# A linear-attention and max-out network kernel: the bonus of the third chunk by corner products, twelve more products of zeros at the start, and a new table of due times

## The chip, the cores and the metric

One NeuronCore of a Trainium2 chip runs the whole program. The metric is device time in microseconds; three runs of the kernel before are known, and one more execution was profiled. TensorE (PE) multiplies, VectorE (DVE), ScalarE (ACT) and GpSimd (POOL) do element work, and SyncE (SP) issues nearly all transfers.

## The reference, cut to what matters

```python
for t in range(S):                         # S = 768, B = 4, H = 8, D = 48
    cur = einsum('bhd,bhe->bhde', u[None] * k[t], v[t])          # the bonus of the own token
    y[t] = einsum('bhd,bhde->bhe', r[t], state + cur)
    state = w[None, :, :, None] * state + einsum('bhd,bhe->bhde', k[t], v[t])
x = y as (3072, 384)
h = maximum(maximum(x @ w1, x @ w2), x @ w3)                     # 384 -> 768
out = h @ w_out                                                  # 768 -> 384
```

## The kernel before, in words

The 768 tokens are cut into 12 chunks of 64. For each chunk the attention forms scores (keys against receptances, 64x64 for each of 32 pairs of batch and head), masks them to the earlier tokens, and multiplies them with the values (`va` in the plan) and the receptances with the running state; `ke` is the product that renews the state. Each chunk is done in two halves, q = 0 and 1. Behind the attention of a chunk comes its network: for six slices f of the hidden layer three products `up` of nine matmuls (128x256, float16), the maximum of the three on ACT and DVE, and then the products `dn`. The float64 weights come as halves (`word`), are turned into float16 high and low parts by DVE and ACT (lines 319 to 330), and an `up` needs the parts of its slice.

Chunks 0 to 3 (`WHOLE`) take the attention in float32 with 64x64 corners of TensorE (`corner`, line 563); from chunk 4 on it is float16 high and low parts (line 476), spread over block-diagonal tiles by transfers.

The score of a token with itself needs the bonus u, and there are two ways to it. In chunks 0 and 1 (`EARLY`) ACT multiplies the keys by u (`rated`, line 485), TensorE forms a second set of corners `bo`, and `mask_bonus` (line 490) copies its diagonal into the tile `amz`, which is zeroed once and used by all early chunks; `mask` (line 502) then copies the scores of earlier tokens into it. In the other chunks the diagonal is made from the token-major tensors: `product` (lines 457 and 458: r times u, times k), `total` (line 462: a sum over 48), and `diagonal` (line 466: spread on the eye), on DVE or POOL, and `mask` goes on top.

Nothing is ordered by the code's own sequence. Every step is given to `Plan.do` with a due time, an engine, a cost, what it reads and writes, and the pools from which it takes buffers. `Plan.order` then fills the engines greedily by these costs, and the steps are recorded in that order, so each engine runs its own list in order. `SHIFT` moves the due times of each kind of step in five stages of the program. A product of zeros (`stir`, line 626) runs on TensorE in four places: once before any data is there, and three times between the first products.

Loads of chunks 0 to 3 go into tiles that later hold spread operands (`blocks[...]room`, named by `FEATS` and `TOKS`) or, where `TOKS` has None, into the pool `tok` of three buffers: halves 2/0, 2/1 and 3/0 fill it in the kernel before.

Of the kernel before, what the change touches and what calls it, by code (L numbers as in the profile page):

```python
# [29 lines left out]
EARLY = (0, 1)  # L30
FEATS, TOKS = ("kd", "kb", "ktd", "ktb"), ("sd", "vb", None, None)
# [15 lines left out]
class Plan:  # L47
# [11 lines left out]
        "act tkl": (0, -13.11, 0, 0, 0), "act tkt": (0, 50.28, 0, 0, 0), "act vdh": (0, 0, 0, -105.14, -53.73), "act wsq": (0, 0, 0, 0, 5.11),
        "act x": (-47.33, 85.49, 26.22, -20.76, -8.91), "act xh": (-44.75, 0, -100.57, -28.3, -1.81), "act xsq": (0, 15.62, 0, -43.66, -14.22),  # L60
        "act ztop": (0, 54.65, 0, 0, 0), "dve a": (0, 0, -5.17, 101.87, 25.76), "dve al": (0, 0, 0, 60.55, 12.26, 0, 0, 0, -22.37, 7.04),
        "dve am": (0, 0, 10.09, -12.88, 8.82, 0, 0, -0.23, -2.17, -8.37), "dve amz": (-64.19, -80.08, -13.83, -77.16, 0),
        "dve ends": (0, 0, 0, 149.19, 0), "dve flag": (0, 0, 0, 0, 113.54), "dve good": (0, 0, 0, 0, 32.48),
        "dve hl": (0, -19.31, 58.16, -54.83, -18.79, 0, 1.9, 5.29, -9.39, 0.06),
        "dve kT": (-10.41, -22.95, 4.53, -23.13, -0.12, -5.93, 16.46, -7.26, 21.08, 0.27),
        "dve kdec": (0, 10.74, 3.61, -55.17, -3.05, 0, 2.89, -4.71, 5.85, 6.5), "dve kdl": (0, 0, 0, 28.7, 76.75, 0, 0, 0, 12.53, -8.95),
        "dve ktdl": (0, 0, 0, -75.87, 22.48, 0, 0, 0, -22.66, 3.88), "dve lo": (0, -60.79, 0, 0, 0), "dve m": (0, -79.26, -57.34, -93.14, 22.59),
        "dve rT": (0.88, -19.98, -13.12, 14.62, -30.28, 11.81, 1.66, -8.46, -9.57, 8.77), "dve rl": (0, 0, 0, -95.56, 15.83, 0, 0, 0, -27.84, 18.29),
        "dve sdl": (0, 0, 0, -36.04, -22.46), "dve state": (0, 14.9, -58.41, 7.59, 26.82), "dve vdl": (0, 0, 0, 26.05, 13.41),
# [148 lines left out]
def kernel(ctx, tc, feat, tok, wu, ut, ws, wo, cst, vz, out):  # L218
# [615 lines left out]
    def weight(n, h, due):  # L834
# [350 lines left out]
```

## Time and profile before

| what | us |
|---|---|
| three runs | 400.0, 399.22, 397.24 |
| median | 399.22 |
| the profiled execution | 398.11 |
| its span, first to last instruction | 395.7 |
| TensorE busy | 375.1 |
| VectorE busy | 256.2 |
| ScalarE busy | 211.2 |
| GpSimd busy | 157.3 |

A busy time is a mean over stages with different limits: TensorE is busy for 95% of the span, but some of that is zeros and some of it ran at half the clock. The rows below show stretches of time, and the granted clock (1.00 is 2.4 GHz, 0.50 is 1.2 GHz) stands in its own column.

### The profile page before, as it was taken

The numbers are of one execution on the slowest core, as the hardware profiler recorded it, in microseconds if no ns is written. First come the engines' busy times: TensorE is split into PE (matmuls) and PEld (weight loads), VectorE is DVE, ScalarE is ACT, GpSimd is POOL, SyncE is SP. The second block draws the span as 40 slices with busy tenths as digits, with TensorE's granted clock in tenths as the row PEclk, the third lists the DMA queues.
The fourth block names the chain that finished last, engine by engine and source line by source line (L and its number), as shares of the span: only waits on it lengthen the run. The fifth ranks groups of instructions, "written<-read, shape, count | busy, mean of one in ns | idle before, by whom it ended". The sixth has DMA issues, their size and how long they took to land.

```text
span 395.7 us, 12676 instructions
## 1 busy us (share of the span) xinstructions
PE 375.1 (95%) x5256; PEld 337.2 (85%) x5256; DVE 256.2 (65%) x495; ACT 211.2 (53%) x532; POOL 157.3 (40%) x154
## 2 busy tenths in 40 slices
PE   6979499899999999999999999899999999999996
PEld 5868398688889998899998899799899999988885
DVE  5629989997646766934377449789467668243441
ACT  4335174676457676544444448457349738922421
POOL 7366764313365839730465116156019104000000
PEclk9999889999999999999999999999999999999999
DMA  7996329964639797876516892994995894420101
GB/s 267 411 407 209 130 67 315 258 221 118 174 92 274 200 244 193 244 198 181 162 59 165 206 288 72 257 277 117 240 314 140 196 250 107 120 65 7 41 3 45
DMA packets 28271, 72.55 MB, mean 183 GB/s; under 512 B 4849, under 2 KB 12081, under 8 KB 28209
## 3 DMA queue, kind: packets, MB, share of 16 engines
q1 hardware_dynamic: 28064, 71.59, 63.5%
q8 instruction: 43, 0.70, 0.8%
q14 instruction: 20, 0.16, 0.2%
q10 hardware_dynamic: 144, 0.10, 0.1%
HBM read 35.97 MB, written 4.72 MB: 103 GB/s over the span
## 4 chain that ended last, share of the span: by engine, by line
PE 72%; DMA 10%; DVE 5%; issue 4%; ACT 3%; SPq 3%; POOL 1%; DVEq 0%; POOLq 0%
PE psm L630 55%; PE psa L563 9%; PE psa L476 8%; DMA ktb<-ktd 4%; DMA sb<-sd 3%; SPq L559 2%; DVE m L649 1%; PE psm L626 1%; DMA feat<-in_feat_dram 1%; DMA kd<-in_feat_dram 1%; DVE raw L323 1%; ACT junk L426 1%; DVE tok L472 1%; DVE hl L655 1%; DMA x<-x 1%
## 5 line engine op out<-in xcount | busy, mean ns | idle before, releaser
L630 PEld LDWEIGHTS <-w 128*128 128x128 f16 x2592 | 250.1, 98 | 33.5 <-issue 2.4
L630 PE MATMUL psm<-x,w 128*128 128x256 f16 x1944 | 220.8, 273 | 3.5 <-DVE m L649 2.5
L649 DVE SCALAR_TENSOR_TENSOR m<-psm,m 128x256 f32<-128x256 f32 x144 | 60.0, 419 | 48.8 <-PE psm L630 46.3
L652 ACT CAST hh<-m 128x256 f16<-128x256 f32 x72 | 28.7, 400 | 54.6 <-DVE m L649 53.9
L630 PE MATMUL psm<-hh,w 128*128 128x256 f16 x432 | 55.8, 273 | 0.0
L655 POOL TENSOR_TENSOR hl<-m,hh 128x256 f16<-128x256 f32 x25 | 17.9, 718 | 85.4 <-ACT hh L652 81.7
L457 POOL TENSOR_TENSOR am<-tok,u_sb 128x384 f32<-128x384 f32 x19 | 22.5, 1185 | 45.8 <-DVE al L512 45.8
L645 ACT ACTIVATE m<-psm 128x256 f32<-128x256 f32 x72 | 27.0, 377 | 24.1 <-PE psm L630 22.8
L630 PE MATMUL psm<-hl,w 128*128 128x256 f16 x216 | 33.4, 273 | 0.0
L554 DVE SCALAR_TENSOR_TENSOR x<-psa,x 128x512 f16<-128x512 f32 (+1 forms) x24 | 16.2, 677 | 26.4 <-ACT x L548 26.2
L655 DVE TENSOR_TENSOR hl<-m,hh 128x256 f16<-128x256 f32 x47 | 24.0, 514 | 8.7 <-ACT hh L652 8.7
L426 ACT ACTIVATE junk<-tok 128x384 bf16<-128x384 f32 x48 | 24.9, 519 | 5.2 <-DMA tok<-in_tok_dram 4.4
L466 POOL TENSOR_TENSOR am<-cs,a 128x512 f32<-128x512 f32 x19 | 21.7, 1140 | 14.9 <-DVE a L462 8.7
L675 ACT ACTIVATE io<-psm 128x256 f32<-128x256 f32 x36 | 12.9, 382 | 26.4 <-PE psm L630 26.4
L438 POOL TENSOR_TENSOR feat<-feat,wrt 128x512 f32<-128x512 f32 x12 | 17.1, 1423 | 21.4 <-DMA feat<-in_feat_dram 21.4
L476 PE MATMUL psa<-rh,sb 128*128 128x64 f16 x256 | 23.6, 193 | 2.0 <-DMA sb<-sd 2.0
L502 DVE COPY_PREDICATED am<-cs,psa 128x512 f32<-128x512 int32 x20 | 14.5, 731 | 16.4 <-PE psa L476 15.5
L548 ACT ACTIVATE x<-psa 128x512 f16<-128x512 f32 (+1 forms) x24 | 14.1, 585 | 20.1 <-PE psa L476 16.4
L476 PE MATMUL psa<-ah,vb 128*128 128x64 f16 x256 | 23.9, 193 | 0.1
L476 PE MATMUL psa<-al,vb 128*128 128x64 f16 x128 | 22.8, 193 | 0.0
L476 PE MATMUL psa<-rl,sb 128*128 128x64 f16 x128 | 22.7, 193 | 0.0
L476 PEld LDWEIGHTS <-sb 128*128 128x128 f16 x384 | 20.0, 98 | 2.2 <-DMA sb<-sd 1.5
(138 smaller groups left out, 572.9 us busy)
## 6 DMA issues: line engine op xcount, KB each, us to landing
tok<-in_tok_dram SPq DMA_DIRECT2D x20, 576.0 KB, 7.5
feat<-in_feat_dram SPq DMA_DIRECT2D x16, 512.0 KB, 6.6
raw<-in_ws_dram SPq DMA_DIRECT2D x12, 576.0 KB, 6.5
out_dram<-io SPq DMA_DIRECT2D x36, 128.0 KB, 3.4
kb<-kd SPq DMA_DIRECT2D x16, 256.0 KB, 4.4
kb<-kd SPq DMA_DIRECT2D x16, 248.0 KB, 4.5
vb<-vd SPq DMA_DIRECT2D x16, 224.0 KB, 5.2
sb<-sd SPq DMA_DIRECT2D x16, 224.0 KB, 5.7
```

Source lines behind the costliest of these rows:

```text
L426: nc.scalar.activation(out=junk[:, 0:U * D].rearrange("p (u d) -> p u d", u=U), in_=src, func=AF.Square, scale=scale, accum_out=stat[:, ki ...
L438: eng.tensor_tensor(out=t[n], in0=t[n], in1=tb, op=ALU.mult)
L457: eng.tensor_tensor(out=w.rearrange("p (g b) d -> p g b d", g=2), in0=t["r"], in1=by_token(u_sb, q), op=ALU.mult)
L466: eng.tensor_tensor(out=t["a"], in0=eye.unsqueeze(1).broadcast_to([P, U, C]), in1=t.pop("sum").unsqueeze(2).broadcast_to([P, U, C]), op=AL ...
L476: nc.tensor.matmul(out=ps, lhsT=l[i], rhs=rr[j], start=first and n == 0, stop=last and n == 2)
L554: nc.vector.scalar_tensor_tensor(out=lo, in0=src, scalar=x_scale(c), in1=hi, op0=ALU.mult, op1=ALU.subtract)
L563: nc.tensor.matmul(out=ps[hh * C + at:hh * C + at + n, i, :], lhsT=lhs[HS[hh]], rhs=rhs[HS[hh]], start=first, stop=last)
L630: nc.tensor.matmul(out=ps, lhsT=a, rhs=b, start=first and n == 0, stop=last and n == len(prods) - 1)
L645: nc.scalar.mul(out=m, in_=ps, mul=by)
L649: nc.vector.scalar_tensor_tensor(out=m, in0=ps, scalar=by, in1=m, op0=ALU.mult, op1=ALU.max)
L652: nc.scalar.copy(out=h[0][:, f, :], in_=m)
L655: eng.tensor_tensor(out=h[1][:, f, :], in0=m, in1=h[0][:, f, :], op=ALU.subtract)
```

## The change

Chunk 2 is added to `EARLY`, so that its bonus comes by corner products, and its tokens are loaded without r, into the room of the tiles `sb` and not into the pool `tok`. The first run of zeros has 32 products in place of 20. The planner's costs of transfers and of GpSimd change, which changes no instruction but the order of all of them, and every entry of `SHIFT` is new.

```diff
-EARLY = (0, 1)
-FEATS, TOKS = ("kd", "kb", "ktd", "ktb"), ("sd", "vb", None, None)
+EARLY = (0, 1, 2)
+FEATS, TOKS = ("kd", "kb", "ktd", "ktb"), ("sd", "vb", "sb", None)
...
-        "act ah": (0, 0, 0, -114.33, 80.6), "act hh": (0, 36.88, -27.4, -16.07, -13), "act his": (0, -118.51, 0, 0, 0),
+        "act ah": (0, 0, 0, -121.52, 105.27), "act hh": (0, 43, 2.68, -4.11, -0.5), "act his": (0, -53.13, 0, 0, 0),
...
-        do(due, eng, n * Plan.ISSUE[eng] + 0.35 * (n == 2), fn, reads, writes, takes, size + n * 3e4, lanes=n)
+        do(due, eng, n * Plan.ISSUE[eng] + 0.35 * (n == 2), fn, reads, writes, takes, size + n * 4.5e4, lanes=n)
...
-        return ("pool", 0.05 + 2.4e-3 * columns)
+        return ("pool", 0.1 + 2.5e-3 * columns)
...
-        dma(due, fetch, 8 * P * HN, takes=[("raw64", w)])
+        dma(due, fetch, 530842, takes=[("raw64", w)])
...
-            dma(due, lambda: load_feat(c, q), 524288, writes=[f])
+            dma(due, lambda: load_feat(c, q), 356516, writes=[f])
...
-        dma(due, lambda: load_tok(c, q), 589824, takes=[("tok", t)])
+        dma(due, lambda: load_tok(c, q), 513147, takes=[("tok", t)])
...
-        dma(due - 0.22, lambda: spread(nc.sync, kb[q], kd[q], C), 681574, reads=[("kdh", q), ("kdl", q)], writes=[("kb", q)], n=2)
+        dma(due - 0.22, lambda: spread(nc.sync, kb[q], kd[q], C), 558891, reads=[("kdh", q), ("kdl", q)], writes=[("kb", q)], n=2)
...
-        do(due, "pe", 1.0 + 1.0 * q, lambda: values_apart(q), reads=[masked(c, q), ("padded", q), *[("va", c, 0)] * q], writes=[("did", 0, q)] + [("xq", 0)] * q, takes=[("psa", ("va", c, q))])
+        do(due, "pe", 1.0 + 1.55 * q, lambda: values_apart(q), reads=[masked(c, q), ("padded", q), *[("va", c, 0)] * q], writes=[("did", 0, q)] + [("xq", 0)] * q, takes=[("psa", ("va", c, q))])
...
-    do(-9, "pe", 4.3, lambda: stir(20), writes=["warm"], takes=[("psm", "warm")])
+    do(-9, "pe", 5.6, lambda: stir(32), writes=["warm"], takes=[("psm", "warm")])
...
-            for name, tenant, at in (("sd", 0, -0.7), ("kd", 0, -0.4), ("kb", 1, -0.39), ("vd", 0, -0.31), ("vb", 1, -0.3), ("sb", 0, -0.29), ("ktd", 2, -0.2), ("ktb", 3, -0.19)):
+            for name, tenant, at in (("sd", 0, -0.7), ("kd", 0, -0.4), ("kb", 1, -0.39), ("vd", 0, -0.31), ("vb", 1, -0.3), ("sb", 2, -0.29), ("ktd", 2, -0.2), ("ktb", 3, -0.19)):
```

The table of due times decides the order, so its rows are shown as the engines' lists. On VectorE, the stretch before the masks of chunk 2 in the kernel before (`amz` belongs to chunk 1, `am` to chunk 2, `raw` and `w` are weights, `ktb` and `feat` the keys of chunks 3 and 4):

```order
L490 COPY_PREDICATED amz_161<-cs,psa 128x512
L323 SCALAR_TENSOR_TENSOR raw_267<-raw_267,ztop_109 128x576
L502 COPY_PREDICATED amz_161<-cs,psa 128x512
L323 SCALAR_TENSOR_TENSOR raw_270<-raw_270,ztop_110 128x576
L330 SCALAR_TENSOR_TENSOR w_98<-raw_267,w_98 128x576
...
L457 TENSOR_TENSOR am<-tok,u_sb 128x384
L458 TENSOR_TENSOR am<-am,tok 128x384
...
L438 TENSOR_TENSOR ktb_150<-ktb_150,wrt 128x512
L466 TENSOR_TENSOR am<-cs,a 128x512
L438 TENSOR_TENSOR feat<-feat,wrt 128x512
L502 COPY_PREDICATED am<-cs,psa 128x512 x2
```

The same stretch of VectorE in the changed kernel (here `am` and `tok` are chunk 3's, and `amz` serves chunk 1 in rows ahead of `w_98` and chunk 2 behind it):

```order
L323 SCALAR_TENSOR_TENSOR raw_265<-raw_265,ztop_109 128x576
L323 SCALAR_TENSOR_TENSOR raw_301<-raw_301,ztop_110 128x576
L490 COPY_PREDICATED amz_160<-cs,psa 128x512
L490 COPY_PREDICATED amz_161<-cs,psa 128x512
L502 COPY_PREDICATED amz_160<-cs,psa 128x512
L502 COPY_PREDICATED amz_161<-cs,psa 128x512
L330 SCALAR_TENSOR_TENSOR w_98<-raw_265,w_98 128x576
...
L472 TENSOR_TENSOR tok<-tok,tkl 128x384 x2
L490 COPY_PREDICATED amz_160<-cs,psa 128x512
L462 TENSOR_REDUCE a<-am 128x8
L502 COPY_PREDICATED amz_160<-cs,psa 128x512
L554 SCALAR_TENSOR_TENSOR x<-psa,x 128x512
```

The first two conversions of weights stand ahead of chunk 1's masks now, both bonus masks stand ahead of the first score mask, and the mask of chunk 2's first half no longer has a scaling of `ktb`, a `diagonal` and a scaling of `feat` right in front of it.

On SyncE, the loads in the middle of the first stage in the kernel before (`tok` are halves 2/0, 2/1 and 3/0, then 3/1 and 4/0 behind the six small transfers of x; `raw` are weight halves):

```order
L300 DMA raw_348<-in_ws_dram 128x2304
L253 DMA vb_152<-in_tok_dram 128x784
L253 DMA tok<-in_tok_dram 128x1152 x3
L244 DMA ktb_150<-in_feat_dram 128x1024
L244 DMA feat<-in_feat_dram 128x1024
...
L559 DMA x<-x 16x2x256 x6
L253 DMA tok<-in_tok_dram 128x1152 x2
L398 DMA kb_147<-kd_139 64x2048
L399 DMA kb_147<-kd_139 64x1984
L300 DMA raw_1005<-in_ws_dram 128x2304
```

And in the changed kernel (`sb` are halves 2/0 and 2/1, the three of `tok` are 3/0, 3/1 and 4/0):

```order
L300 DMA raw_326<-in_ws_dram 128x2304
L253 DMA vb_152<-in_tok_dram 128x784
L253 DMA sb_153<-in_tok_dram 128x784
L253 DMA sb_154<-in_tok_dram 128x784
L253 DMA tok<-in_tok_dram 128x1152 x3
L244 DMA ktb_150<-in_feat_dram 128x1024
L244 DMA feat<-in_feat_dram 128x1024 x2
...
L559 DMA x<-x 16x2x256 x6
L300 DMA raw_1002<-in_ws_dram 128x2304
L300 DMA raw_1036<-in_ws_dram 128x2304
```

No load of tokens stands behind the transfers of x any more, and the next weight halves follow them directly.

On TensorE the first `up` (`w_98` is the weight tile of slice 0) moves ahead of the scores of chunk 2 and the state product of chunk 1, which stood in front of it before; of the difference, the place behind the values of chunk 1's first half:

```order
 L563 MATMUL psa<-amz_160,vb_151 64x64 x2
 L563 MATMUL psa<-kb_147,state 48x64 x2
+L630 LDWEIGHTS w_98
+L630 MATMUL psm<-x,w_98 128x256
...
 L563 MATMUL psa<-ktd_141 64x64 x16
+L630 LDWEIGHTS w_99
```

Three `up` of slice 0 stand there now ahead of the scores of chunk 2 (`ktd_141`), and three of slice 1 (`w_99`) behind them. The bonus products of chunk 2 follow later, one of them behind the values of chunk 1's second half, since both use the same tile `amz`.

## Rows read from the trace of the kernel before

**Rows 1.** Busy time of each engine by stretch, with granted clock, DMA share, GB/s
```profile
33.81:43.97 10.16, 10.14 (x185) 8.95 (x182) 10.06 (x18) 3.07 (x7) 7.42 (x8) 1.00 0.85 283
43.97:49.97 6.00, 0.01 (x1) 0.04 (x1) 5.99 (x8) 1.07 (x3) 4.89 (x5) 0.66 0.06 14
49.97:100.00 50.03, 47.44 (x701) 42.27 (x702) 44.74 (x78) 32.40 (x66) 19.35 (x18) 0.97 0.66 196
100.00:392.50 292.50, 289.45 (x3777) 262.31 (x3774) 176.67 (x355) 159.59 (x429) 106.36 (x101) 1.00 0.63 166
392.50:395.74 3.24, 0.00 (x0) 0.00 (x0) 0.00 (x0) 0.38 (x1) 0.00 (x0) 1.00 0.16 51
```

**Rows 2.** All engines in order of time, 43.5 to 50 us
```profile
44.96 1.45 POOL L438 TENSOR_TENSOR ktb<-ktb,wrt 128x512 f32<-128x512 f32 x1
45.20 1.75 DVE L438 TENSOR_TENSOR ktb<-ktb,wrt 128x512 f32<-128x512 f32 x1
46.37 1.71 POOL L438 TENSOR_TENSOR feat<-feat,wrt 128x512 f32<-128x512 f32 x1
46.88 1.75 DVE L466 TENSOR_TENSOR am<-cs,a 128x512 f32<-128x512 f32 x1
48.54 0.68 DVE L438 TENSOR_TENSOR feat<-feat,wrt 128x512 f32<-128x512 f32 x1
49.15 1.33 DVE L502 COPY_PREDICATED am<-cs,psa 128x512 f32<-128x512 int32 x2
49.97 0.37 PE L563 MATMUL psa<-am,tok 64*64 64x64 f32 x2 [6.01 <-issue]
```

**Rows 3.** VectorE in order of time, 27 to 43.5 us
```profile
27.73 0.73 DVE L490 COPY_PREDICATED amz<-cs,psa 128x512 f32<-128x512 int32 x1 [4.72 <-PE psa L563]
31.66 0.76 DVE L330 SCALAR_TENSOR_TENSOR w<-raw,w 128x576 f16<-128x576 f32 x1
...
41.17 1.16 DVE L457 TENSOR_TENSOR am<-tok,u_sb 128x384 f32<-128x384 f32 x1
42.36 0.56 DVE L458 TENSOR_TENSOR am<-am,tok 128x384 f32<-128x384 f32 x1
...
43.17 0.54 DVE L462 TENSOR_REDUCE a<-am 128x8 f32<-128x384 f32 x1
```

**Rows 4.** TensorE's busy time and granted clock in single steps
```profile
9.47:11.78 2.31, 2.31 (x14) 0.50 1.05 411
26.58:27.68 1.10, 1.10 (x44) 1.00 1.09 432
49.97:53.27 3.30, 3.30 (x71) 0.58 0.00 0
53.09:55.10 2.01, 2.01 (x78) 1.00 0.03 8
```

**Rows 5.** TensorE in order of time, its first products and its first `up`
```profile
1.00 4.26 PE L626 MATMUL psm<-still 128*128 128x256 f16 x20 [1.00 <-POOL still L307]
5.83 0.66 PE L373 MATMUL psa<-cs,hl 128*128 128x128 f32 x4 [0.57 <-DVE hl L361]
7.90 1.63 PE L563 MATMUL psa<-kd 64*64 64x64 f32 x32 [1.41 <-POOL kd L438]
...
24.40 1.27 PE L626 MATMUL psm<-still 128*128 128x256 f16 x10
...
29.32 0.33 PE L563 MATMUL psa<-amz,vb 64*64 64x64 f32 x4 [0.71 <-PE psa L563]
...
33.81 4.10 PE L630 MATMUL psm<-x,w 128*128 128x256 f16 x36
```

**Rows 6.** SyncE's issues in order of time, 40 to 62 us
```profile
41.28 3.94 SPq L559 DMA_DIRECT2D x<-x  x6
56.09 2.50 SPq L253 DMA_DIRECT2D tok<-in_tok_dram  x2
```

**Rows 7.** Who waited for whom: us in total, times, longest
```profile
DVE am L502 <- PE psa L476: 15.5, 9, 6.0
```

More of the change, by code (lines that the diff above doesn't have):

```diff
@@ L59 @@
[L59 to L67, printed above, removed]
@@ new lines @@
+        "act io": (0, 0, -76.11, -7, 36.16), "act kdh": (0, 0, 0, 49.77, -0.37), "act ktdh": (0, 0, 0, 70.24, -35.65),
+        "act m": (0, -50.94, 81.17, -98.46, 13.13), "act pr": (-33.9, -40.95, -18.85, 33.14, 0), "act rh": (0, 0, 0, -20.72, 14.16),
+        "act sdh": (0, 0, 0, -173.35, 159.62), "act sq": (0, 0, 0, -92.18, -22.37), "act state": (0, 210.3, 0, 0, 0), "act tke": (0, 197.16, 0, 0, 0),
+        "act tkl": (0, -73.87, 0, 0, 0), "act tkt": (0, 60.98, 0, 0, 0), "act vdh": (0, 0, 0, -130.83, -91.08), "act wsq": (0, 0, 0, 0, 27.33),
@@ new lines @@
+        "act x": (-47.62, 113.61, -12.22, -33.02, -2.09), "act xh": (-38.17, 0, -93.98, -38.26, -8.48), "act xsq": (0, 10.5, 0, -45.95, -22.08),
+        "act ztop": (0, 15.06, 0, 0, 0), "dve a": (0, 0, -5.17, 88.09, 43.39), "dve al": (0, 0, 0, 70.41, -0.76, 0, 0, 0, -19.77, 6.9),
+        "dve am": (0, 0, 10.09, 6.47, -3.1, 0, 0, -0.23, -1.4, -8.29), "dve amz": (-59.16, -132.68, -47.62, -77.16, 0),
+        "dve ends": (0, 0, 0, 163.55, 0), "dve flag": (0, 0, 0, 0, 183.16), "dve good": (0, 0, 0, 0, 51.62),
@@ new lines @@
+        "dve hl": (0, -2.84, 79.75, -50.29, -8.93, 0, 2.85, -0.35, -16.16, 2.6),
+        "dve kT": (-22.04, -58.9, -21.24, -11.14, -1.44, -24.02, 3.14, -8.4, 24.17, 0.32),
+        "dve kdec": (0, -0.93, -10.41, -52.06, -4.6, 0, 4.23, -3.13, 0.18, 11.63), "dve kdl": (0, 0, 0, 11.58, 100.01, 0, 0, 0, 15.39, -13.36),
+        "dve ktdl": (0, 0, 0, -78.34, 25.86, 0, 0, 0, -21.05, 7.84), "dve lo": (0, -22.33, 0, 0, 0), "dve m": (0, -69.8, -49.52, -90.01, 28.78),
+        "dve rT": (5.74, -21.81, -2.03, 5.37, -39.77, 8.82, 16.7, -6.07, -15.17, 6.21), "dve rl": (0, 0, 0, -86.72, 19.44, 0, 0, 0, -23.56, 27.14),
@@ L80 @@
+        "dve sdl": (0, 0, 0, -60.81, -10.43), "dve state": (0, 21.03, -31.69, 15.44, 22.09), "dve vdl": (0, 0, 0, 23.72, 22.55),
[4 rows of a table added]
+        "pool amz": (-251.34, 0, 0, 0, 0), "pool kb": (0, 0, 0, -70.52, 0), "pool kdh": (0, 0, 0, -167.05, 0), "pool ktb": (0, 0, 0, 32.41, 0),
+        "pool ktdh": (0, 0, 0, -2.98, 0), "pool sb": (0, 0, 0, 90.02, 0), "pool sdh": (0, 0, 0, -173.98, 0), "pool vb": (0, 0, 0, -17.59, 0),
[4 rows of a table added]
     }
@@ L851, in fetched @@
         if c in WHOLE:
-            dma(due, lambda: load_feat(c, q), 524288, writes=[f])
+            dma(due, lambda: load_feat(c, q), 356516, writes=[f])
             if not c:
-                dma(due, lambda: load_padded(q), 4 * P * NV[q], writes=[("padded", q)])
-            n = 4 * P * (3 * TK if c not in EARLY else 2 * TK + 16 if c else TK + 16)
+                dma(due, lambda: load_padded(q), 3 * P * NV[q], writes=[("padded", q)])
+            n = 3.5 * P * (3 * TK if c not in EARLY else 2 * TK + 16 if c else TK + 16)
             dma(due + (0 if c else 2.0), lambda: load_tok(c, q), n, **(dict(writes=[t]) if TOKS[c] else dict(takes=[("tok", t)])))
             return
-        dma(due, lambda: load_feat(c, q), 524288, takes=[("feat", f)])
-        dma(due, lambda: load_tok(c, q), 589824, takes=[("tok", t)])
+        dma(due, lambda: load_feat(c, q), 356516, takes=[("feat", f)])
+        dma(due, lambda: load_tok(c, q), 513147, takes=[("tok", t)])
     def squares(c, q, due):
@@ L894, in before_mask @@
             return
-        do(due - 0.16, "dve", 2 * dve(U * D) + 0.13, lambda eng: product(eng, c, q), reads=[t], takes=[("am", ("am", c, q))], writes=[("kdec", c, q)], near=1, also=("pool", 2 * pool(U * D)[1] + 0.2))
+        do(due - 0.16, "dve", 2 * dve(U * D) + 0.13, lambda eng: product(eng, c, q), reads=[t], takes=[("am", ("am", c, q))], writes=[("kdec", c, q)], near=1, also=("pool", 2 * pool(U * D)[1] + 0.5))
         do(due - 0.08, "dve", dve(U * D), lambda: total(c, q), reads=[("am", c, q)], takes=[("a", ("a", c, q))])
@@ L1059, in part @@
                 do(due + 0.02, "act", act(TOK), lambda: do_tile(("io", c, m), leaving(banks[m], TOK, SC_O)), reads=[bank], takes=[("io", ("io", c, m))])
-                dma(due + 0.03, lambda: nc.sync.dma_start(out=out[m, :, c * TOK:(c + 1) * TOK], in_=T["io", c, m]), 131072, reads=[("io", c, m)])
+                dma(due + 0.03, lambda: nc.sync.dma_start(out=out[m, :, c * TOK:(c + 1) * TOK], in_=T["io", c, m]), 117965, reads=[("io", c, m)])
         most, rest = range(NF - 1), [NF - 1]
```

7 lines of the change are left out of this document (removed), and 16 rows, old and new, of the table SHIFT.

## The prediction

> **What bounds the kernel now.** I read the table of stretches first [rows 1]. From its first `up` at 33.81 us [rows 5] to 392.5 TensorE is busy for 347.04 us out of 358.69 (the sum of the first four rows). The rest is idle: 6.0 in one hole from 43.97 to 49.97, 2.59 between 49.97 and 100, 3.05 in the 292.5 us behind that, 0.02 ahead of the hole. Behind its last product 3.24 us pass. So behind 100 us TensorE is the bound and any kernel with the same products needs nearly the same time; what an order can win lies ahead of 100 us: the hole, the 2.59, and the 33.81 us before the network begins.
>
> Then the hole. It ends when VectorE has put the scores of chunk 2 under the mask at 49.15, and TensorE starts on chunk 2's values at 49.97 [rows 2]. VectorE wasn't idle there: 5.99 us of the 6.0 are busy [rows 1], and in front of the masks stand a scaling of chunk 3's keys (1.75), the `diagonal` (1.75) and a scaling of chunk 4's keys (0.68). The two long ones ran while GpSimd worked (1.45 from 44.96, 1.71 from 46.37); the same scaling without GpSimd takes 0.68. The hole has a second price: the granted clock falls to 0.50, so that chunk 2's first values take 3.30 us at a mean of 0.58, the second 2.01 at 1.00 [rows 4]. That is 1.3 more, and 7.3 in all.
>
> **The change part by part.** My sum has four terms: when the first `up` starts, TensorE's work from there, its idle time from there, and the end. It is made against the profiled 398.11 us, of which 395.74 is the span and 2.37 lies around it; the median of the runs is 1.11 above it.
>
> *Bonus of chunk 2.* Gone are two `product` (one on VectorE, 1.16 + 0.56, one on GpSimd), two `total` of 0.54 and two `diagonal` (one on VectorE, 1.75) [rows 2, 3]: 4.55 us of VectorE. New are two masks of 0.73 [rows 3], so VectorE is relieved by 3.1 us, all of it ahead of the masks where the hole was. TensorE gets two sets of corners at 1.1 [rows 4]: 2.2 us that lie on its path, since it has no idle time to hide them. ScalarE gets two `rated`; it is busy for 1.07 of the 6.0 us of the hole [rows 1], so I cost them at nothing; without that cover they would cost their length, under 1 us each, once. Since all early chunks share one tile, the second bonus mask of chunk 2 comes only behind chunk 1's second values. In the new list TensorE still has chunk 2's first values and one `ke` between that product and the second values, 2.0 + 1.1 us, against two masks of 0.73: hidden.
>
> *More zeros.* The first run ends at 5.26, and the first scores start at 7.90, when GpSimd has scaled the keys; those take 1.63, and the ten zeros behind them 2.31 at a clock of 0.50, against 1.10 and 1.27 for the same at 1.00 [rows 4, 5]. Twelve more zeros take 1.5 to 2.6 us (0.127 each from the later run, 0.213 from the first), so they and the four transposes (0.66) end between 7.4 and 8.5. If the clock then stays at 2.4 GHz the start gains 0.5 + 1.0 = 1.5; if not, up to 0.6 is lost. What is late next is the load: transfers fill their engines there (DMA share 1.05 [rows 4]), and chunk 1's second half is asked for two loads of 0.52 MB later, at 411 GB/s 2.6 us. It is the fourth product in line behind the others, and I see some 5 us of cover. I take 1.5, with ends at -0.6 and 1.5.
>
> *First network products earlier.* The scores of chunk 2 and the `ke` of chunk 1, 1.1 each, move behind them. Against that, chunk 1's first values waited only 0.71 for their mask [rows 5], and now wait for both bonus masks and their own: one product later and one mask more, +0.75. The two conversions of weights that stood between the masks (about the 0.76 of the step behind them, each) move ahead into VectorE's 4.72 us of idle time [rows 3]; so the first weight part (0.76 behind the masks) is there before these values end. First `up`: 33.81 - 2.2 - 1.5 + 0.75 = 30.9, with ends at 30.0 and 33.0.
>
> *TensorE's work from there*: 347.04 - 1.3 (clock) + 2.2 (moved behind) + 2.2 (bonus) = 350.1.
>
> *Idle time from there.* Without the hole it was 2.59 + 3.05 + 0.02 = 5.7. Does the hole close? VectorE's list from the first bonus mask of chunk 1 to the score mask of chunk 2's first half was 30 steps (27.73 to 49.87, the ends of this stretch in rows 3 and 2); at the durations that each kind has without GpSimd beside it they sum to 17.3 us of the 22.1, and 4.5 of the rest are seven steps drawn out beside GpSimd (1.07 for the scaling in rows 2). In the new list the same stretch has 25 steps, 14.2 us. It starts at 27.73 - 1.5 = 26.2 and ends at 40.4, with the same 4.5 of losses at 44.9. TensorE gets to these values at 30.9 + six `up` (36 matmuls take 4.10 [rows 5], so 6.0) + 2.0 of values + six other sets at 1.05 = 45.2. So the hole closes, with almost nothing to spare: the weight parts of slice 1 come as closely ahead of their `up`, and short waits, not long enough for the clock to fall, are likely. Against these: SyncE stood at a token load from 45.22, the end of the transfers of x, to 56.09 [rows 6], since the three buffers were full until chunk 2's `ke`; the weights behind it came late, and part of the 2.59 is waiting for weights. Chunk 2's tokens now lie elsewhere, and the next weight loads follow x at once. I let the two cancel: 5.7, with ends at 3 and 12.
>
> Sum: 30.9 + 350.1 + 5.7 + 3.24 = 389.9 us of span, + 2.37 = 392.3, and at the level of the median 393.4 us, 1.5% below 399.22.
>
> **The rivals.** *VectorE takes the place of the hole.* It is busy for 44.74 of the 50.03 us behind it [rows 1]; if TensorE comes 8 us earlier to the same conversions, it meets them half done. For it: the losses beside GpSimd, and that the new lists put products of chunk 3 and maxima in front of chunk 2's masks. Price: the 4.5 us of losses once more, as waiting, which gives 398; it decides as soon as the 0.3 us to spare is gone. A page of the Trainium skill states this mechanism (SBUF — State Buffer, "SBUF: two separate sides"): a VectorE instruction with two SBUF inputs and a GpSimd instruction that reads SBUF lock the shared port, and the later one waits for the whole of the other. The trace agrees, with 1.75 beside 0.68 [rows 2], while masks, which read PSUM, kept 0.73. By that rule the new bonus masks are exempt and the removed `product` and `diagonal` were not, which speaks for the change; the moved scalings and hl steps are not exempt.
>
> *The hole stays*, because chunk 2's values wait for something other than their own bonus (the state, or the order of the list): +6.0 + 1.3, which gives 400.7, no difference.
>
> *Slower: values right behind their scores.* In the new list the four values of chunks 4 and 5 stand 4.6, 9.3, 3.7 and 7.3 us of products behind their scores, where before they stood 32, 44, 6.6 and 28.6 behind. Between the two lie a mask (0.73), a high part on ScalarE and a low part on GpSimd, some 2.6 us if nothing is queued before them. If VectorE's queue delays these masks by the 4.2 us that stood before them in rows 2, TensorE waits 2.2 and 3.1 us in two of the four places, 398.7; at 6.3 us of queue it waits 11.1 in three, which gives 404.5. From 6 us on it decides. Against it: VectorE waited for scores of the float16 stage in 9 places, 15.5 us in all [rows 7], so its queue was empty there, and it is busy for 177 of the 292.5 us behind 100.
>
> **How the numbers follow.** The forecast, with the hole mostly closed, has 0.58, and a still better one (TensorE almost without waits, 389 to 391) 0.11; VectorE as the bound 0.16; the hole stays 0.09; slower 0.06. A measurement of this kernel tells about 1% from no change (395.2 to 403.2). Faster takes the first two and a little of the third: 0.72 (the third's price begins at nothing). Same takes the rest of these and the staying hole: 0.22. Slower: 0.06. For the range: the low end is a start at 30.0 and 3 us of idle time, 389.8, less 1 because three runs of one kernel lay 2.8 us apart; the high end takes in the first rival, 398.
>
> **What would show it.** Right: one run of `up` begins near 31 us; no idle stretch of TensorE over 3 us behind 30; the clock at 1.00 from about 5 us to the end; two more corner products of 1.1 and no line 466 before chunk 3; SyncE's weight loads directly behind x. Wrong: a wait of several us for line 490 or 502, a clock of 0.50 between 30 and 60 us, or idle time over 3 us behind 100 in front of line 476.

## The result, and the profile after

The changed kernel takes 395.06 us (median of 8 executions, 391.91 to 396.12). The kernel before, run beside it, takes 399.61 (8 executions, 396.97 to 402.69). The ratio is 0.9881, with a 95% interval of 0.9835 to 0.9926: 1.2% less time. Ratios here and below leave out executions that were disturbed, medians don't. The forecast was 393.4, its range 388.8 to 398.0. The profiled execution took 395.43 us, with a span of 393.6.

Stretches of the changed kernel: length, busy time of PE, PEld, DVE, ACT and POOL with their instructions, granted clock, DMA share, GB/s. The first row begins at the first `up`, the last at the end of TensorE's last product.

```profile
30.90:43.97 13.07, 12.29 (x249) 10.96 (x246) 12.93 (x19) 6.18 (x15) 10.42 (x9) 1.00 0.72 271
43.97:100.00 56.03, 53.84 (x780) 47.67 (x781) 48.15 (x85) 33.38 (x69) 22.88 (x23) 1.00 0.55 159
100.00:149.36 49.36, 49.36 (x661) 44.37 (x659) 27.99 (x54) 26.12 (x74) 20.20 (x22) 1.00 0.71 178
149.36:152.42 3.06, 0.00 (x1) 0.03 (x2) 0.00 (x0) 0.81 (x4) 0.67 (x1) 1.00 1.02 270
152.42:158.80 6.38, 6.38 (x62) 5.16 (x63) 2.88 (x6) 3.93 (x11) 1.21 (x1) 0.73 0.70 183
158.80:390.48 231.68, 230.10 (x3041) 208.50 (x3039) 145.70 (x300) 125.34 (x334) 69.47 (x64) 1.00 0.62 162
390.48:393.56 3.08, 0.00 (x1) 0.00 (x0) 0.00 (x0) 0.38 (x1) 0.00 (x0) 0.87 0.17 55
```

Against [rows 1]: from 43.97 to 100 us TensorE idles for 2.19 us, where the hole alone was 6.0 and the rest 2.59. The clock stays at 1.00 there. But a new row has come in, 3.06 us without a product at 149 us, and behind it 6.38 us at a mean clock of 0.73. From the first `up` to the last product TensorE idles for 7.61 us (11.65 before) and is busy for 351.97 (347.04 before).

TensorE in order of time; the wait ahead of a product and what ended it stand in brackets.

```profile
0.99 6.59 PE L626 MATMUL psm<-still 128*128 128x256 f16 x32 [0.99 <-POOL still L307]
7.95 1.15 PE L563 MATMUL psa<-kd 64*64 64x64 f32 x32
9.96 1.26 PE L626 MATMUL psm<-still 128*128 128x256 f16 x10
...
28.93 0.33 PE L563 MATMUL psa<-amz,vb 64*64 64x64 f32 x4 [1.48 <-issue]
...
30.90 3.12 PE L630 MATMUL psm<-x,w 128*128 128x256 f16 x27
...
44.44 1.14 PE L563 MATMUL psa<-vb 64*64 64x48 f32 x32 [1.11 <-DVE amz L490]
46.49 0.28 PE L563 MATMUL psa<-amz,sb 64*64 64x64 f32 x4
...
152.42 0.76 PE L476 MATMUL psa<-vd,ktb 128*128 128x48 f16 x24 [3.06 <-DMA ktb<-ktd]
```

The first scores take 1.15 us and the zeros behind them 1.26, where they took 1.63 and 2.31 [rows 4, 5]. The first `up` is at 30.90. Chunk 2's values (`amz,sb`) start at 46.49 without a wait, and stood at 49.97 behind a wait of 6.01 [rows 2]. The last row is the new wait: chunk 5's first state product, for the spread keys `ktb`.

VectorE in the place of the former hole [rows 2], and GpSimd beside it.

```profile
40.54 3.20 DVE L472 TENSOR_TENSOR tok<-tok,tkl 128x384 f32<-128x384 f32 x2
43.67 0.72 DVE L490 COPY_PREDICATED amz<-cs,psa 128x512 f32<-128x512 int32 x1
44.29 0.53 DVE L462 TENSOR_REDUCE a<-am 128x8 f32<-128x384 f32 x1
44.74 0.72 DVE L502 COPY_PREDICATED amz<-cs,psa 128x512 f32<-128x512 int32 x1
...
47.19 0.88 DVE L438 TENSOR_TENSOR feat<-feat,wrt 128x512 f32<-128x512 f32 x1
48.00 0.72 DVE L490 COPY_PREDICATED amz<-cs,psa 128x512 f32<-128x512 int32 x1
```

```profile
40.51 1.28 POOL L438 TENSOR_TENSOR ktb<-ktb,wrt 128x512 f32<-128x512 f32 x1
41.74 1.59 POOL L438 TENSOR_TENSOR feat<-feat,wrt 128x512 f32<-128x512 f32 x1
...
44.18 1.16 POOL L448 TENSOR_TENSOR rl<-feat,rh 128x512 f16<-128x512 f32 x1
```

The masks of chunk 2's first half are done at 45.46, 1.0 us before they are needed. What is left of the hole is the 1.11 us in front of 44.44: the two `decay` steps (line 472) ahead of the first mask took 3.20 us, while such a step took 0.54 at 30.67 us, and GpSimd ran two scalings from 40.51 to 43.33. The Trainium skill (SBUF — State Buffer, "SBUF: two separate sides") has a VectorE instruction with two SBUF inputs and a GpSimd instruction that reads SBUF lock a shared port pair against each other, for the whole instruction. The trace agrees: the `decay` steps have two SBUF inputs, and the mask at 44.74, which reads its scores from PSUM, kept its 0.72 beside a GpSimd step. The mask of 0.73 that the prediction read as a sign of this [rows 3] ran while GpSimd stood idle, and showed nothing of it.

GpSimd's last step on the keys of the new wait, and SyncE's issues ahead of it.

```profile
135.67 0.91 POOL L413 TENSOR_TENSOR ktd<-tok,ktd 128x384 f16<-128x384 f32 x1
```

```profile
135.98 0.96 SPq L244 DMA_DIRECT2D feat<-in_feat_dram  x1
137.84 0.46 SPq L398 DMA_DIRECT2D vb<-vd  x1
...
139.03 0.67 SPq L253 DMA_DIRECT2D tok<-in_tok_dram  x1
139.80 0.84 SPq L398 DMA_DIRECT2D sb<-sd  x1
...
141.33 1.29 SPq L398 DMA_DIRECT2D ktb<-ktd  x1
...
145.49 0.47 SPq L398 DMA_DIRECT2D ktb<-ktd  x1
```

GpSimd had finished the low part of these keys at 136.58. The transfer was issued 4.75 us later, behind a `vb` and an `sb` that TensorE needs at 172.17 and a `tok` of chunk 6, and TensorE had its data at 152.42.

### The profile page after: what moved, and what is told of

The parts are those of the page before. It is cut to its first block, busy times and chain, and to the rows that moved or that the text cites. A ratio compares the mean times of both kernels' runs of the same rounds, so it can differ in the third digit from the quotient of the medians.

```text
span 393.6 us, 12822 instructions
## 1 busy us (share of the span) xinstructions
PE 378.6 (96%) x5332; PEld 339.3 (86%) x5332; DVE 258.1 (66%) x503; ACT 211.9 (54%) x536; POOL 142.6 (36%) x140
## 4 chain that ended last, share of the span: by engine, by line
PE 77%; DMA 8%; DVE 7%; issue 3%; SPq 2%; ACT 2%; POOL 0%; DVEq 0%; POOLq 0%
PE psm L630 58%; PE psa L476 10%; PE psa L563 7%; PE psm L626 3%; DMA raw<-in_wo_dram 3%; DMA ktb<-ktd 2%; DMA kb<-kd 2%; DMA vb<-vd 1%; DVE raw L323 1%; DVE m L649 1%; DVE w L330 1%; SPq L559 1%; DVE tok L472 1%; SPq L398 1%; DVE hl L655 1%
## 5 line engine op out<-in xcount | busy, mean ns | idle before, releaser
L630 PE MATMUL psm<-hh,w 128*128 128x256 f16 x432 | 56.9, 276 | 0.0
L655 POOL TENSOR_TENSOR hl<-m,hh 128x256 f16<-128x256 f32 x26 | 20.9, 807 | 75.9 <-ACT hh L652 75.9
L457 POOL TENSOR_TENSOR am<-tok,u_sb 128x384 f32<-128x384 f32 x13 | 14.4, 1104 | 64.0 <-DMA tok<-in_tok_dram 56.2
L630 PE MATMUL psm<-hl,w 128*128 128x256 f16 x216 | 34.2, 277 | 0.3 <-DVE hl L655 0.3
L655 DVE TENSOR_TENSOR hl<-m,hh 128x256 f16<-128x256 f32 x46 | 24.9, 547 | 11.5 <-ACT hh L652 11.5
L466 POOL TENSOR_TENSOR am<-cs,a 128x512 f32<-128x512 f32 x17 | 19.3, 1133 | 16.9 <-DVE a L462 14.2
L529 DVE SCALAR_TENSOR_TENSOR state<-state,wc,psa 128x192 f32<-128x192 f32 x36 | 13.1, 404 | 13.7 <-PE psa L476 13.5
L476 PEld LDWEIGHTS <-vb 128*128 128x128 f16 x384 | 20.7, 98 | 1.0 <-issue 0.8
L438 DVE TENSOR_TENSOR feat<-feat,wrt 128x512 f32<-128x512 f32 x21 | 17.2, 831 | 5.8 <-DMA feat<-in_feat_dram 5.8
```

The costliest lines, as they stand in the source:

```text
L438: eng.tensor_tensor(out=t[n], in0=t[n], in1=tb, op=ALU.mult)
L457: eng.tensor_tensor(out=w.rearrange("p (g b) d -> p g b d", g=2), in0=t["r"], in1=by_token(u_sb, q), op=ALU.mult)
L466: eng.tensor_tensor(out=t["a"], in0=eye.unsqueeze(1).broadcast_to([P, U, C]), in1=t.pop("sum").unsqueeze(2).broadcast_to([P, U, C]), op=AL ...
L476: nc.tensor.matmul(out=ps, lhsT=l[i], rhs=rr[j], start=first and n == 0, stop=last and n == 2)
L630: nc.tensor.matmul(out=ps, lhsT=a, rhs=b, start=first and n == 0, stop=last and n == len(prods) - 1)
L655: eng.tensor_tensor(out=h[1][:, f, :], in0=m, in1=h[0][:, f, :], op=ALU.subtract)
```

## The experiments

Each ratio is to the kernel before, run on the same chip. The changed kernel stands in the first line.

| kernel | median us | ratio | 95% interval |
|---|---|---|---|
| the change | 395.06 | 0.9881 | 0.9835 to 0.9926 |
| ve_back | 399.75 | 0.9994 | 0.9959 to 1.0028 |
| masks_first | 398.26 | 0.9947 | 0.9910 to 0.9985 |
| bonus_alone | 456.08 | 1.1398 | 1.1340 to 1.1456 |
| zeros20 | 394.54 | 0.9859 | 0.9814 to 0.9904 |
| ktb_first | 395.71 | 0.9895 | 0.9842 to 0.9947 |
| k_both | 394.84 | 0.9896 | 0.9848 to 0.9944 |
| k_both_z20 | 396.84 | 0.9892 | 0.9858 to 0.9926 |
| k_both_mask | 395.20 | 0.9845 | 0.9799 to 0.9891 |
| sp3 | 391.55 | 0.9805 | 0.9756 to 0.9854 |
| sp3_z20 | 392.35 | 0.9840 | 0.9790 to 0.9890 |
| sp3_bo2 | 390.84 | 0.9756 | 0.9708 to 0.9804 |
| sp_best | 389.99 | 0.9775 | 0.9732 to 0.9817 |

Where two ratios are compared below, the uncertainty of their difference is the root of the sum of squares of their half intervals. "Lag" is the start of a product in one profiled execution less that of the same product in another; a negative lag is called a lead. Each is read from one execution of each kernel, while the times are medians of 6 to 12.

**ve_back: VectorE's work put back**

```diff
+    def extra():        # 128x384 products as L457 and L458, two sums as L462, one product on the eye
+        ...
     order = plan.order(...)
+    order.insert(148, dict(also=None, fn=extra))    # ahead of chunk 2's first bonus mask
```

> The changed kernel with five instructions put back on VectorE, directly ahead of chunk 2's first bonus mask: two products of 128x384, two sums, and one product on the eye, of the sizes that the kernel before had there for chunk 2 (their result goes into a scratch tile and is not used). Some 3.5 us of work, 4.5 beside GpSimd. Theory (the relief of VectorE is what closed the hole): the wait of 1.11 us in front of chunk 1's second state product grows to 4.6 to 5.6 us, the clock falls to 0.50 behind it, and at 55 us TensorE is 3.5 to 5.5 us later than in the changed kernel. Of this 1 to 3 us are made up for by 165 us (the waits between 60 and 80 us and the one for ktb are then shorter), so 0.8 to 3.5 us slower at the end. Rival (VectorE was not what held these products): less than 1.5 us later at 55 us, and no difference at the end.

TensorE's product behind the wait in this kernel:

```profile
48.11 1.94 PE L563 MATMUL psa<-vb 64*64 64x48 f32 x32 [3.69 <-DVE amz L490]
```

And its stretch from there (PE alone, then clock, DMA share, GB/s):

```profile
48.11:54.60 6.49, 6.49 (x137) 0.57 0.07 14
```

The wait grew from 1.11 to 3.69, the products behind it ran at 0.57, and chunk 2's values came 5.1 us later than in the changed kernel; 1.1 of that stood there ahead of the wait, from the start. Of the 5.1 us 2.2 were made up by chunk 5's state product, where the wait for `ktb` was still 2.29; 4.3 us of lag stood again at 327 us. The time is that of the kernel before. The five instructions took 3.84 us, so work of this size on VectorE in this place is enough to decide the whole gain. This kernel has the new due times and the 32 zeros too, so these alone, with VectorE as full as this, gave nothing that could be measured. The ratio lies 0.0113 above the changed kernel's, uncertain by 0.0057: 4.5 us, where 0.8 to 3.5 were expected, and the upper part of that isn't excluded.

**masks_first: the kernel before, with chunk 2's masks ahead of two scalings**

```diff
 order = plan.order(...)
+order.insert(147, order.pop(150))   # first mask of chunk 2 ahead of the diagonal
+order.insert(149, order.pop(152))   # second mask
+order.insert(149, order.pop(145))   # scaling of ktb behind them
```

> The kernel before with two scalings moved on VectorE, and nothing else: the scaling of ktb (chunk 3's keys) and that of feat (chunk 4's keys), which stood ahead of chunk 2's two masks, follow them, and the first mask stands ahead of the diagonal of the second half. Theory (the hole is the time of the steps ahead of the mask, whichever they are): the first mask ends near 46 us instead of 49.86, the hole shrinks from 6.0 to about 2.1 us, the clock falls for a shorter time or not at all, and 4 to 5.3 us are gained without any change of the bonus: 394.3 to 395.6, ratio 0.987 to 0.990. Rival (VectorE is the bound behind the hole too, so work put off is waited for later): the scalings that were put off, 1.75 and 0.68 us, are waited for between 50 and 100 us, and 1.5 us or less are gained, ratio over 0.996.

TensorE's larger waits in this kernel:

```profile
44.91 0.48 PE L563 MATMUL psa<-am,tok 64*64 64x64 f32 x4 [2.06 <-issue]
...
56.27 8.48 PE L630 MATMUL psm<-x,w 128*128 128x256 f16 x74 [1.11 <-DVE w L330]
...
74.18 0.81 PE L630 MATMUL psm<-x,w 128*128 128x256 f16 x6 [1.54 <-DVE m L649]
```

Its stretch behind the first of them:

```profile
44.91:48.34 3.43, 3.43 (x68) 0.56 0.00 1
```

The hole shrank to 2.06 as expected, and chunk 2's values came 5.06 us earlier than before, 1.1 of it from the start, where the clock stayed up in this execution. But the clock still fell behind the wait (these values took 3.43 us against 3.30 [rows 4]). By 57 us the lead was 2.6, with 1.57 lost in waits for weight parts from VectorE, and nothing of it was left at chunk 5's second state product at 154.7. The way there can be followed: ScalarE stood for 4.83 us until the scaling of `feat` that had been put off was done at 48.12, earlier than before by no more than the 1.1 of the start; its casts of weights came behind that, and VectorE waited 1.29 us for two of these. The time is 0.5% less than before: 2.1 us, uncertain by 1.5, which rules out the 4 to 5.3 of the theory and is near the 1.5 of the rival. The mechanism is that of my first rival: VectorE takes the place of the hole. Here work put off on VectorE was waited for.

**bonus_alone: the kernel before with the bonus by corners, old costs, due times and zeros**

```diff
-EARLY = (0, 1)
+EARLY = (0, 1, 2)        # with TOKS and the tenant of sb as in the change
```

> The kernel before with chunk 2's bonus by corner products (and its tokens in the room of sb), but 20 zeros and the old costs and due times, from which the lists are made anew. Theory (the hole is VectorE's work for the bonus in front of chunk 2's masks): no idle stretch of TensorE over 2 us between 40 and 55 us, no clock of 0.50 there; minus 7.3 for the hole, plus 2.2 for the products, and with a first up near 33.8 as before: 394 to 396 us, ratio 0.985 to 0.991. Rival (what closed the hole are the new lists, the bonus only makes room): the hole or a wait of the same length elsewhere stays, and the time is 399 to 402, ratio 0.997 to 1.006.

Two stretches of it (PE alone):

```profile
33.00:51.20 18.20, 18.04 (x442) 1.00 0.69 235
51.20:120.00 68.80, 54.57 (x570) 0.85 0.50 146
```

SyncE's issues in it:

```profile
39.85 0.43 SPq L244 DMA_DIRECT2D feat<-in_feat_dram  x1
47.60 0.56 SPq L398 DMA_DIRECT2D vb<-vd  x1
...
51.15 1.85 SPq L300 DMA_DIRECT2D raw<-in_ws_dram  x2
```

TensorE's first large wait:

```profile
59.20 5.03 PE L630 MATMUL psm<-x,w 128*128 128x256 f16 x27 [5.12 <-ACT w L326]
```

The hole is gone (0.16 us idle between 33 and 51) without the new costs and due times. The lists were made anew, though, and the two scalings that stood ahead of the masks in [rows 2] aren't there either, so that this run doesn't show the bonus alone. And both expectations missed the time by over 50 us: the old due times no longer fit. SyncE stood from 40.28 to 47.60 in front of a `vb`, the weight loads behind it came late, and TensorE waited for weight parts, later for x. What the new table of due times is worth can't be split from the bonus by this run, and no run has the new table with the old bonus; without a fitting table the bonus is a large loss.

**sp3_bo2: the bonus products run twice.** It stands on sp3, below.

```diff
-        for i in range(U):
+        for _ in range(2 if name == "bo" and c == 2 else 1):
+            for i in range(U):
```

> The kernel with the four moves on SyncE, and both sets of bonus products of chunk 2 run twice (the second overwrites the first with the same values): 2 x 1.1 us more on TensorE. It prices the 2.2 us of bonus products that the prediction put on TensorE's path. Rival (the prediction's own term: TensorE has no idle time to hide them): everything behind 48 us is 2.2 us later, and the time 2.0 to 2.4 us longer than with the four moves alone. Theory (between 40 and 52 us TensorE waits for VectorE's masks, 1.32 us before chunk 2's second values, so products there are partly hidden): 0.8 to 1.2 us later at 55 us, and 0.4 to 1.2 us longer at the end.

Chunk 2's second values came 0.88 us later than in sp3, though the first `up` was 1.28 later by the spread of the start, and the time was no longer: the difference of the ratios is -0.0049, uncertain by 0.0069. The 2.2 us that the rival wanted are 0.0055, outside of it. So the bonus products are hidden here, in whole or for the most part.

**zeros20: 20 zeros in the changed kernel's lists**

```diff
-    do(-9, "pe", 5.6, lambda: stir(32), ...)
+    do(-9, "pe", 5.6, lambda: stir(20), ...)
```

> The changed kernel with 20 products in the first run of zeros instead of 32, and every list as in the changed kernel. Theory (the zeros keep the clock up until the first scores): the zeros end near 5.3 us, the clock falls to 0.50 ahead of the first scores, these and the ten zeros behind them take 1.63 and 2.3 us instead of 1.15 and 1.27, and the first up starts at 32.0 to 32.4 instead of 30.9; up to 1.5 us slower than the changed kernel, ratio to the kernel before 0.990 to 0.992 where the changed kernel has 0.988. Rival (the start is set by loads, not by the clock): the lost 1.5 us are taken up by waits for data further on, the first up within 0.4 us of 30.9, and the time as the changed kernel's.

TensorE in this kernel:

```profile
7.73 1.15 PE L563 MATMUL psa<-kd 64*64 64x64 f32 x32 [1.32 <-POOL kd L438]
...
24.29 2.32 PE L626 MATMUL psm<-still 128*128 128x256 f16 x10
...
33.12 1.05 PE L630 MATMUL psm<-x,w 128*128 128x256 f16 x8
...
152.39 0.78 PE L476 MATMUL psa<-vd,ktb 128*128 128x48 f16 x24 [2.22 <-DMA ktb<-ktd]
```

The start came later, as the theory wanted (33.12 against 30.90), but not by its mechanism: the first scores ran at full clock, and the slow zeros are those of 24.29. The 2.2 us shrank to 1.42 by 67 us, to 0.75 by 77, and were gone at the wait for `ktb`. The time is the changed kernel's, as the rival said; the first `up` isn't, against the rival. What this run alone doesn't show: with 32 zeros the first scores took 1.15 us in all eight profiled executions on record, with 20 zeros 1.15 in three and 1.63 to 1.97 in three (before, bonus_alone, sp3_z20). That speaks for the theory's mechanism in some executions; the counts are small.

**ktb_first, k_both, sp3: the transfers in front of the new wait**

```diff
 order = plan.order(...)
+order.insert(537, order.pop(555))   # ktb_first: chunk 5's first ktb behind feat 6/0
+order.insert(563, order.pop(578))   # k_both, in addition: the second ktb behind its low part,
+order.insert(563, order.pop(550))   #   and sb 1 behind that
+order.insert(590, order.pop(610))   # sp3, in addition: x of chunk 4 ahead of chunk 2's outputs
```

> The changed kernel with one transfer moved on SyncE: the spreading of the keys of chunk 5, first half (ktb), stands directly behind the load of feat of chunk 6 and ahead of one vb, one tok and one sb, which it followed. Theory (the wait of 3.06 us in front of this chunk's ke, and the clock of 0.50 behind it, come from the transfer's place in SyncE's list): it is issued near 137 us instead of 141.3 and lands near 148 instead of 152.3; no idle time over 0.5 us at 149 us, the clock stays at 1.00, and 4 to 4.7 us are gained on the changed kernel: 390.4 to 391.5, ratio 0.976 to 0.980. Rival (the transfer engines are full there, with a share of 1.02 to 1.04, so the order only passes the wait on): a wait of 2 us or more for vb, sb, ktb or feat within the next 40 us, and less than 1.5 us gained.

Waits of ktb_first between 140 and 170 us (us in total, times, longest):

```profile
PE psa L476 <- DMA ktb<-ktd: 1.9, 1, 1.9
PE psm L630 <- DVE m L649: 0.5, 1, 0.5
```

The first transfer was issued at 137.42, and its product didn't wait. TensorE led the changed kernel by 3.9 us at 155, and by 0.1 at 163: the second `ktb`, now issued at 148.30, was waited for, and the clock fell to 0.62 for 4.29 us behind that. The rival's wait came, if not by its reason, as the next run shows.

> The changed kernel with three transfers moved on SyncE: both spreadings of chunk 5's keys (ktb) stand ahead now, the first directly behind the load of feat of chunk 6, the second ahead of one sb, one feat and one tok. Moving the first alone took away the 3.06 us of waiting and the slow clock in front of it, 3.9 us of lead at 155 us, and lost them again by 163 us to a wait of 1.93 for the second and a clock of 0.50 behind that. Theory (the wait is a matter of which transfer goes first; those passed have time): the second is issued near 143 us instead of 148.3, no wait over 0.5 us for either, and the lead of 3.5 to 4.5 us on the changed kernel holds to the end: 390.5 to 391.5, ratio 0.977 to 0.981. Rival (between 135 and 155 us the transfer engines are full, and whatever goes last is waited for): a wait of 1.5 us or more for feat, sb, tok or vb before 200 us, and under 1.5 us gained.

SyncE's issues in k_both:

```profile
148.98 7.76 SPq L1060 DMA_DIRECT2D out_dram<-io  x3
156.79 4.82 SPq L559 DMA_DIRECT2D x<-x  x6
```

TensorE's waits in k_both:

```profile
161.87 0.38 PE L630 MATMUL psm<-x,w 128*128 128x256 f16 x2 [2.01 <-DMA x<-x]
162.90 2.69 PE L630 MATMUL psm<-x,w 128*128 128x256 f16 x23 [0.65 <-DMA x<-x]
```

Neither `ktb` was waited for. The lead was 5.7 us at 152 and 2.4 at 164: the network of chunk 4 waited for x, whose six transfers stood behind an output that waits for chunk 2's last product. The theory of one misplaced transfer fell, and so did the rival's reason: no full transfer engine passed this wait on (the DMA share was 0.36 between 150 and 165 us), a second place in the list did.

> The kernel with both spreadings of chunk 5's keys (ktb) ahead, and in addition the six small transfers of chunk 4's x ahead of the outputs of chunk 2. In the runs with the two spreadings alone the lead of 5.5 us at 151 us shrank to 2.4 by 164 us: the first up of chunk 4 waited 2 to 3 us for x, whose six transfers stood on SyncE behind an output that waits for chunk 2's last product, though x was complete since 139 us. Theory (three places in SyncE's list, each taken out by its own move): x lands before 155 us, no wait over 0.5 us between 140 and 170 us, 4.5 to 5.5 us less than the changed kernel: 389.5 to 390.5, ratio 0.974 to 0.978. Rival (the transfer engines are full and pass the wait on once more): a wait of 2 us or more before 210 us, for kb, vb, sb or feat, and under 1.5 us gained.

SyncE's issues in sp3:

```profile
145.70 5.43 SPq L559 DMA_DIRECT2D x<-x  x6
151.69 6.66 SPq L1060 DMA_DIRECT2D out_dram<-io  x6
```

Two stretches of sp3:

```profile
140.00:165.00 25.00, 25.00 (x339) 22.83 (x337) 13.99 (x28) 13.12 (x38) 10.41 (x10) 1.00 0.75 202
165.00:384.00 219.00, 216.32 (x2828) 196.17 (x2826) 139.93 (x285) 119.40 (x319) 65.55 (x61) 1.00 0.63 163
```

No idle time from 140 to 165 us, and the lead of 6.1 us at 152 holds for the most part: 4.9 at the values of chunk 11. The ratio is 0.0076 below the changed kernel's, uncertain by 0.0067: 3.0 us, uncertain by 2.7, where 4.5 to 5.5 were expected.

**k_both_z20 and sp3_z20: 20 zeros on these two**

> The same three transfers moved, and 20 zeros instead of 32. With 20 zeros the first up came 2.2 us later, but the lag shrank to 0.75 us by 78 us and to nothing at the wait for ktb. Theory (what the start gains is lost in later waits for data: some 1.4 us of it ahead of 80 us, the rest at the wait for ktb): without that wait the remaining 0.75 us stays to the end, so 0.5 to 1.0 us slower than the same with 32 zeros. Rival (the start counts in full once the wait for ktb is gone): 1.5 to 2.2 us slower than with 32 zeros.

> The same four moves on SyncE, with 20 zeros instead of 32. Theory (with the waits behind 140 us gone, what remains of the 2.2 us at the start stays: 0.75 us by 78 us): 0.5 to 1.0 us slower than the same with 32 zeros. Rival (the start counts in full): 1.5 to 2.2 us slower. Second rival (another wait further on takes it up): no difference.

The first `up` stood at 33.7 us (in an execution of 400.90, far above that kernel's median) and 33.9. The three pairs with 32 and 20 zeros differ in ratio by -0.0022, -0.0004 and +0.0035; their mean is 0.1 us, uncertain by 1.5. The rival that has the start count in full (2.2 us) is out; whether 0 or 1 us stays is not settled.

**k_both_mask and sp_best: chunk 1's masks in another order, and two more transfers**

```diff
+order.insert(91, order.pop(93))       # score mask of 1/0 ahead of the bonus mask of 1/1
+order.insert(770, order.pop(779))     # sp_best, on sp3: kb of 7/1 ahead of an output and a load,
+order.insert(1285, order.pop(1290))   #   and vb of 10/0
+order.insert(1285, order.pop(1283))   #   ahead of kb 11/1
```

> The same three transfers moved, and on VectorE the score mask of chunk 1's first half ahead of the bonus mask of its second half. Theory (the 1.48 us before chunk 1's values is the wait for two masks that are not needed yet; VectorE has time): that wait shrinks to 0.1, the first up starts near 29.6 us, or at 30.1 where it waits for its weight part; but most of the 0.8 to 1.4 us is lost by 80 us, as with the zeros, and the time is that of the same kernel without this move to within 0.7 us. Rival (each us saved in front of the first up comes through): 1.0 to 1.5 us faster than without this move.

> The same four moves on SyncE, the score mask of chunk 1's first half ahead of the bonus mask of its second half on VectorE, one kb of chunk 7 ahead of an output and a load, and one vb of chunk 10 ahead of a kb. Theory (each is a transfer or a mask that is waited for, behind one that has time): the wait of 1.5 us before chunk 1's values is gone, the ones of 0.3 to 1.2 us for kb near 207 us and of 0.4 to 1.6 us for vb near 323 us are under 0.3, and it takes 1.5 to 3 us less than with the four moves alone: 387 to 389, ratio 0.968 to 0.973. Rival (small waits are taken up by each other): within 1 us of the kernel with the four moves alone.

In k_both_mask the wait of 1.48 was gone, the first `up` stood at 28.78, 3.2 us ahead of k_both. At chunk 5's first state product 1.1 us of that were left. At 161 us, where k_both waited for x, TensorE now waited 3.03, 0.83 and 0.90 us with the clock at 0.50 between 164 and 166, and the lead on the changed kernel went from 6.9 to 0.1 us (from 5.7 to 2.4 in k_both). Its ratio is 0.0051 below k_both's, uncertain by 0.0066. sp_best is the fastest kernel with a reason for each move: 389.99 us, 2.25% less than the kernel before. Its ratio is 0.0106 below the changed kernel's, uncertain by 0.0062. Against sp3 the gain of 0.003 can't be told from none. Its profiled execution took 395.31 us, 5.3 above its median, so that its waits say little of the moves.

## Why the prediction was right, and where not

**The first `up`** at 30.9: the profiled execution has 30.90. That is partly luck: six profiled executions with the same lists up to there have it at 30.90, 31.58, 31.69, 32.01, 32.12 and 32.87. Most of the spread is the clock behind the wait of 1.48 (1.00 in the first two, 0.57 to 0.66 between 29 and 33 us in the others), a price that the prediction didn't have. The base varied as well: masks_first, with the lists of the kernel before up to there, has its first `up` at 32.70 and not at 33.81. Of the parts, the masks cost 0.77 more waiting (1.48 against 0.71 [rows 5], forecast 0.75), and the zeros gave 1.9 us of the start by medians (33.71 in the three runs with 20 zeros on these lists, 31.85 in the six; forecast 1.5), but in two of these three not at the first scores.

**The hole** closed, with 1.11 us left, and the clock stayed up. VectorE was through with the score mask of chunk 2's first half at 45.46, forecast 44.9. The cause that I gave, VectorE's work ahead of the masks, is shown by putting it back (ve_back): a wait of 3.69 us with its clock costs 4.5 us of the time, uncertain by 2.3. The 7.3 us for the whole hole were not measured by themselves.

**TensorE's work from there**: 350.1 forecast, 351.97 measured. Of the difference 1.5 us are one `dn` that took 3.61 us at a clock of 0.56 behind the new wait, where it takes 2.13.

**Idle time**: 5.7 forecast, 7.6 measured. Without the 3.06 at 149 us it would be 4.6. The "short waits" ahead of 100 us are there (1.11, 0.40, 0.39, 0.22, 0.51). The 3.06 is over the bound that the prediction set ("no idle stretch of TensorE over 3 us behind 30"), it is in front of line 476, where its list of signs of being wrong had it, and the clock fell behind it.

**The step that failed** is in the first part: "behind 100 us TensorE is the bound and any kernel with the same products needs nearly the same time; what an order can win lies ahead of 100 us". The new lists lost 4.6 us at 149 us (3.06 + 1.5), and four moves on SyncE won 3.0 us back, uncertain by 2.7. I looked at the new order behind 100 us for the rival of chunks 4 and 5, but only at masks; of the transfers I followed those of the first 60 us. The order showed `ktb` behind `vb`, `tok` and `sb`; I didn't ask which of these TensorE needs first.

**The bonus as 2.2 us on TensorE's path** is mis-sized: run twice, it cost nothing that could be measured. VectorE's masks still set the pace from 40 to 52 us: in ktb_first, k_both and sp3 the first `up` came 0.7 to 1.2 us later than in the changed kernel, and chunk 2's values 0.2 to 0.4 us earlier. The second masks, "hidden" in the prediction, were waited for 0.19 us in the changed kernel and 1.3 in these three.

**The sum** came to 389.9 of span and was 393.6, 3.7 too low. The time was 1.7 too low only, and that is luck: I had added 3.5 us for what lies around the span and for the median, and the changed kernel's median is 1.5 above its profiled span.

**The rivals.** VectorE in the place of the hole: true for a hole that is only moved (masks_first), not for this change. The hole stays: no. Values of chunks 4 and 5 waiting for their scores: no such wait; what idled in front of line 476 was a state product waiting for a transfer.

## What to carry to other kernels

A hole that ends with a busy engine closed here when work was taken from that engine, and mostly moved when work was only put off. An us saved at the start is worth what the next wait for data leaves of it: find that wait, and follow for each transfer of the new order what it was put behind and when each of these is needed. When a misplaced transfer is put right, look for the next one before judging the gain: here the first move and the first three gave nothing that could be measured, and all four some 3 us.

## What the runs showed of the hardware

The granted clock falls behind some waits and not behind others of the same length: behind the 1.48 us at 28.9 the same products ran at 1.00 in the changed kernel (2.04 us) and at 0.55 in k_both (3.49 us); behind 2.06 us in masks_first it fell to 0.56, behind 2.01 us in k_both it stayed at 1.00. The clock isn't all of the spread between executions: two of the changed kernel took 391.91 and 396.12 us at mean clocks of 0.998 and 1.000.

With 20 zeros on the new lists it also fell behind a wait that ended at 23 to 24 us, in all three profiled executions (0.66 to 0.73 from 24 to 29 us), with 32 behind the same wait in one of eight (0.56, the 395.31 us of sp_best). In that wait TensorE stands for nothing that the traces show, and at a fixed place of its list: behind the third product of `kb` in all eight (0.33 to 2.18 us), behind the fifteenth with 20 zeros (1.51 to 1.78), which is the same number of products from the start, since twelve zeros are gone. The transfer engines were full there (a share of 1.01 to 1.02 from 20 to 24 us). What it stands for isn't settled.

The transfer engines are as full with much less moved when spreads run. Two stretches of the changed kernel (PE alone, then clock, DMA share, GB/s), the first with loads only, the second with spreads among them:

```profile
24.89:27.45 2.56, 1.37 (x38) 1.00 1.01 403
135.00:155.00 20.00, 16.94 (x204) 0.97 1.03 247
```

A spread of `ktb` needed a median of 10.5 us from issue to landing in the second, and 5.9 us over the whole program.
